# Moving a weight load behind the first z tile, and storing the last zeta in pieces

## The chip, the cores and the metric

The kernel runs on one core of a Trainium2 chip. The metric is device time in microseconds, smaller being better. The engines are named as in the profile: PE (TensorE, matmul), PEld (its weight loads), DVE (VectorE), ACT (ScalarE), POOL (GpSimd) and SP (SyncE, which here only issues DMA transfers).

## The reference

A filter in the frequency domain is followed by a feed-forward layer with squared ReLU:

```
X = rfft(x, axis=1)                     # x: 8 x 3008 x 256
y = irfft(X * (filt_r + 1j*filt_i), n=3008, axis=1)
h = maximum(y.reshape(24064, 256) @ w_in, 0)      # w_in: 256 x 2048
out = (h * h) @ w_out                              # w_out: 2048 x 256
```

## The kernel before

The Fourier transform of length 3008 = 64 x 47 is done as matrix products in stages, in half precision with sums in single precision. For each of the eight batches:

- `unit_a` is the transform over the 47 points (PE, L347), copied out by ACT (L353) and DVE (L359) into tiles `u`, and stored by `write_u` (SP, L330) to the scratch array `dU` in DRAM; `read_u` (SP, L403) reads it back in another layout as `ut`.
- `unit_b` multiplies by the twiddle factors and sums over 32 points (PE, L412, `psB`); DVE multiplies the result by the filter `sF` into `prod` (L420).
- `unit_p` is the first inverse stage (PE, L457, `psP`), copied by ACT into `ze` and stored to the scratch array `dZ`; `read_z` (SP, L475) reads this back as z tiles `zt`, two half tiles for each of four columns c.
- `unit_y` is the last inverse stage (PE, L493, `psY`), copied by ACT (L500) or DVE (L502) into `yt`, the input of the feed-forward layer.

The feed-forward layer works on 47 groups of 512 tokens. `ffn_g1` (PE, L523) multiplies by W_in; ACT applies the ReLU into `h` (L527); DVE squares it (L534). The product with W_out is done for all groups but the last with seven block products (`products`, PE, L638) in place of eight. They need sums of blocks of W_out, made once by `make_t` (DVE, L590), and sums of blocks of `h` for each group (`sums`, DVE, L609 to L618). Both halves of W_out stand in one tile `sWout`, and the first `make_t` reads from both.

In the main loop the steps of one batch's transform lie between the matmuls of the groups before it, in an order that a planner (`fft_plan`) fixes when the kernel is built. Ahead of that loop stands a prologue written out by hand. It has the first batch's transform with nothing to overlap, and then `unit_a` of batch 1. Batch 0 there has a form of its own: `unit_b` writes its twelve products into a ring (`prods`, five slots), and `unit_p0(k)` for k = 0 to 5 takes two of them at a time (PE, L443), which ACT copies (L445) and SP stores (L446). After it follow:

- `read_z(0, 0)` and `read_z(0, 1)`, SP. The first half of a z tile needs the stores of k = 0 to 2, the second half all six.
- a copy of one element of the first z tile on POOL, `tiny` (L790). It does nothing but hold back what stands behind it on POOL until the first half of that tile has landed.
- a load of W_out's second half, `load_wout(1)` (POOL, L321); the first half, `load_wout(0)`, is issued earlier in the prologue, behind the loads of x for batch 1 and ahead of the seven casts of W_in (`cast_win`, L315).
- `unit_a` of batch 1 for c = 0 to 3; its copies stand on ACT and DVE behind the last zeta.
- thirteen matmuls on zeros, the filler (PE, L796), and then `unit_y(0, 0)` to `unit_y(0, 3)`, each with two small matmuls on zeros ahead (L491).

[...] SP's transfers run through one DMA queue (q1 in the profile), POOL's through another (q0), on the same sixteen DMA engines.

Of the kernel before, what the change touches and what calls it, by code (L numbers as in the profile page):

```python
# [110 lines left out]
def kernel(  # L111
# [9 lines left out]
    nc = tc.nc  # L121
    B, S, D = x.shape
# [32 lines left out]
    dZ = [dram.tile([NM * 96, D], F16, name=f"dZ{b}") for b in range(B)]  # L155

    def psF(name):
        return pps.tile([128, 512], F32, tag="psF", name=name, bufs=2)

    def psO(name):  # L160
        return pps.tile([128, 2, 256], F32, tag="psO", name=name, bufs=2)

    def psH(name):
        return pps.tile([128, 2, 512], F32, tag="psH", name=name, bufs=2)
# [21 lines left out]
    def load_x(b, k):  # L186

        c, h = divmod(k, 2)
        if h == 0:
            x16s[(b, c)] = p_x16.tile([112, 8, D], F16, tag="x16", name=f"x16_{b}_{c}")  # L190
        t = x16s[(b, c)]
        n = 48 if b + 1 < B else N2
        v = xrows[b * S:b * S + 64 * n, :].rearrange("(n h m) d -> h n m d", h=2, m=NM)[h]
        for p0, p1 in ((0, n),) if n == 48 else ((0, 32), (32, n)):
            nc.gpsimd.dma_start(out=t[64 * h + p0:64 * h + p1],  # L195
                                in_=v[p0:p1, 8 * c:8 * c + 8, :])
# [24 lines left out]
    def cast(eng, out, in_):  # L221
        (eng.copy if eng is nc.scalar else eng.tensor_copy)(out=out, in_=in_)
# [38 lines left out]
    sF = const.tile([128, 2, NC, D], F16, name="sF")  # L261
    nc.vector.memset(sF[:, 0, 0:2, :], 0.0)
    ps = psO("warm").rearrange("p a d -> p (a d)")
# [49 lines left out]
    def cast_win():  # L313
        for t, k, c in wins:
            nc.gpsimd.tensor_copy(out=sWin[:, k, c], in_=t)  # L315
# [3 lines left out]
    def load_wout(k):  # L319
        c = slice(8 * k, 8 * k + 8)  # L320
        nc.gpsimd.dma_start(out=sWout[:, c, :],  # L321
                            in_=moe_w_out.rearrange("(jt r) c -> r jt c", r=128)[:, c, :])
# [83 lines left out]
    def unit_b(b, p):  # L406
        if b == 0 and p % 4 > 1:
            ps = psO(f"psB_{b}_{p}").rearrange("p a d -> p (a d)")
        else:
            ps = psF(f"psB_{b}_{p}")  # L410
        for i in range(2):
            nc.tensor.matmul(ps[:, i * D:(i + 1) * D], sSB[:, 2 * p + i, :],  # L412
                             uts[b][:, 2 * p + i, :], start=True, stop=True)
        if b == 0:
            if p == 0:
                prods["ring"] = p_y.tile([128, 5, 2, 2, D], F16, tag="yt", name="prods_0")
            prod = prods["ring"][:, p % 5]
        else:
            prod = p_prod.tile([128, 2, 2, D], F16, tag="prod", name=f"prod_{b}_{p}")
        nc.vector.tensor_mul(  # L420
            out=prod,
            in0=ps.rearrange("p (a d) -> p a d", d=D).unsqueeze(1).to_broadcast([128, 2, 2, D]),
            in1=sF[:, :, 2 * p:2 * p + 2, :])
        prods[(b, p)] = prod
        if b > 0:
            for i in range(2):
                nc.gpsimd.dma_start(out=prod[64 * i:64 * i + 64, 0],  # L427
                                    in_=prod[64 - 64 * i:128 - 64 * i, 1],
                                    accum_op=mybir.AluOpType.add)
# [3 lines left out]
    def unit_p0(k):  # L433

        if k == 0:
            zes[0] = p_h2.tile([128, NC, D], F16, tag="h2", name="ze_0")
        ze = zes[0][:, 4 * k:4 * k + 4, :]
        ps = psH(f"psP_0_{k}")
        for i in range(4):
            c2 = 4 * k + i  # L440
            prod = prods[(0, c2 // 2)]
            for v, w in enumerate((sSP[:, c2, :], sSPx[c2 // 12][:, c2 % 12, :])):
                nc.tensor.matmul(ps[:, i // 2, (i % 2) * D:(i % 2) * D + D], w,  # L443
                                 prod[:, v, i % 2, :], start=(v == 0), stop=(v == 1))
        nc.scalar.copy(out=ze, in_=ps.rearrange("p t (a d) -> p (t a) d", d=D))  # L445
        nc.sync.dma_start(  # L446
            out=dZ[0].rearrange("(s p) d -> p s d", p=128)[:, 4 * k:4 * k + 4, :],
            in_=ze)

    def unit_p(b, p):  # L450
        c, i6 = divmod(p, 3)
# [212 lines left out]
    def fft_plan():  # L664

        fixed, units, moves = [], [], []
        for b in range(1, B):
            f = (b * S // TG) * SLOTS - (48 if b > 1 else 40)
            d = 0
            if b == 1:  # L670
                for n in range(4, 16):
                    fixed.append(((n if n < 8 else n + 2 if n < 12 else 2 * n - 7) + n % 2 / 2,
                                  unit_y, 0, n))
                moves.append((7.5, read_z, 0, 3))
                moves.append((0, read_u, b))
                d = 7
            else:
                for a in range(16):
                    if a % 2 == 0 and b > 2:
                        moves.append((f + ((-57 + 2.3 * a) if b == 3 else (-66 + 2.75 * a)),  # L680
                                      load_x, b, a // 2))
                    if a % 4 == 3:
                        units.append((f + ((-13, -9, -5.5, -3)[a // 4], -46 + 2.1 * a, -56 + 2.75 * a)[min(b, 4) - 2],
                                      unit_a, b, a // 4))
                moves.append((f + (2 if b == 2 else -6.5), read_u, b))
            for p in range(12):
                r = 12 + 16.5 * p / 11 if b == 1 else 6 + 28 * p / 11 if b == 2 else -2 + 36 * p / 11
                units.append((f + r, unit_b, b, p))
                if b == 1 and 2 <= p < 10:
                    moves.append((f + r, load_x, 2, p - 2))  # L690
                units.append((f + r + (4.5 if b == 1 else 7 - 2.5 * p / 11), unit_p, b, p))
            for c in range(4):
                moves.append((f + (40 + d / 14, 43, 48, 54)[c] - d, read_z, b, c))
            for n in range(16):
                (fixed if n < 4 else units).append((f + YN[n] - d, unit_y, b, n))
        work, used, done = {}, set(), {}
        for r, *u in fixed:
            h = int(2 * r)
            used.add(h)
            work.setdefault(h, []).append(u)  # L700
        rank = (unit_a, unit_b, unit_p, unit_y)
        for r, *u in sorted(units, key=lambda u: (rank.index(u[1]), u[0])):
            after = done.get((u[0], u[1]), -1)
# [62 lines left out]
    for k in range(6):  # L766
# [5 lines left out]
        if k < 4:  # L772
            load_x(1, 2 * k)
            load_x(1, 2 * k + 1)
    load_wout(0)
    cast_win()
    for k in range(7):
        if k < 6:
            unit_b(0, 2 * k)
            if k < 5:  # L780
                place_f(1, k + 1, nc.scalar)
            unit_b(0, 2 * k + 1)
        if k > 0:
            unit_p0(k - 1)
        if k < 2:
            place_f(0, k + 4, nc.scalar)
# [1 line left out]
    read_z(0, 1)  # L788
    tiny = const.tile([1, 1], F16, name="tiny")
    nc.gpsimd.tensor_copy(out=tiny, in_=ztiles[0][0:1, 0, 0:1])  # L790
    load_wout(1)
    for c in range(4):
        unit_a(1, c)
    ps = psF("fill")
# [11 lines left out]
    for s in range((NG + 1) * SLOTS):  # L806
        g, k = divmod(s, SLOTS)
# [16 lines left out]
        while stores and stores[0][0] <= s:  # L824
            _, i, n, ost = stores.pop(0)
# [31 lines left out]
```

## Time and profile before

| what | value |
|---|---|
| time, median of 4 runs | 760.9 us |
| the four runs | 760.24, 761.57, 761.99, 760.09 us |
| profiled execution | 760.24 us, span 758.4 us |
| granted TensorE clock, mean | 0.995 |
| busy share of the span: PE / DVE / ACT / POOL | 97% / 86% / 74% / 25% |
| chain that ended last, by engine | PE 88%, DVE 5%, DMA 3%, ACT 2% |
| moved by DMA | 106.36 MB, mean 140 GB/s |

The span is the stretch in the trace from the first to the last instruction; the execution's time is 1.84 us longer. All times inside the kernel below are counted from the start of the span. A busy engine need not be the one that decides: what counts in a stretch is which wait ends last there. The shares above are means over the whole kernel, most of which is the main loop, whereas the edits lie in the first 60 us or so, where the stages have other limits.

### The profile page before, as it was taken

Reading aid. Unit: us, or ns where it says so; the run is one execution under the profiler, and the core shown is the slowest. Engines: PE = TensorE matmul, PEld = TensorE weight load, DVE = VectorE, ACT = ScalarE, POOL = GpSimd, SP = SyncE. Lnnn points to the kernel's source line nnn. Section 1 sums busy time; section 2 is a strip of 40 time slices with the busy share of each in tenths; the row PEclk is TensorE's granted clock in tenths of the full one; section 3 lists DMA queues with packets and bytes.
Section 4 is the critical chain, followed back from the end, with each engine's and each line's share of the span. In section 5 each row is a group of like instructions: output and inputs, shape, how many; then the busy total and the mean of one; then the engine's idle time right before and its main releaser. Section 6 shows DMA issues by size and latency. Waiting matters only on the chain.

```text
span 758.4 us, 20196 instructions
## 1 busy us (share of the span) xinstructions
PE 737.9 (97%) x8511; PEld 536.1 (71%) x8511; DVE 655.8 (86%) x729; ACT 564.7 (74%) x807; POOL 190.7 (25%) x265
## 2 busy tenths in 40 slices
PE   7889999999999999999999999999999999999998
PEld 5535666767777777877678776777767777777776
DVE  5859998899899898989979998999988989888783
ACT  5767788777878777787777778777776777777773
POOL 2810750244222321232304224133311222000000
PEclk9899999999999999999999999999999999999999
DMA  9995898666785557746586547754446334321011
GB/s 350 303 203 161 143 182 232 167 115 119 165 221 122 95 129 169 188 103 137 105 208 139 125 99 137 231 127 102 101 119 184 90 71 98 98 84 44 30 57 57
DMA packets 103459, 106.36 MB, mean 140 GB/s; under 512 B 10320, under 2 KB 93520, under 8 KB 102216
## 3 DMA queue, kind: packets, MB, share of 16 engines
q1 hardware_dynamic: 83928, 81.83, 35.9%
q0 software_dynamic: 19296, 23.05, 21.9%
q8 instruction: 67, 1.10, 0.6%
q10 hardware_dynamic: 144, 0.18, 0.1%
q14 instruction: 24, 0.20, 0.1%
HBM read 57.80 MB, written 48.23 MB: 140 GB/s over the span
## 4 chain that ended last, share of the span: by engine, by line
PE 88%; DVE 5%; DMA 3%; ACT 2%; issue 1%; SPq 1%; DVEq 0%; ACTq 0%
PE psH L523 40%; PE psX L638 20%; PE psY L638 16%; PE psB L412 3%; PE psY L493 2%; PE psP L457 2%; PE psA L347 2%; DMA zt<-dZ 2%; DVE prod L420 1%; DMA xw<-in_x_dram 1%; PE psO L543 1%; ACT h L527 1%; DVE h L534 1%; PE psf L286 1%; PE psP L443 1%
## 5 line engine op out<-in xcount | busy, mean ns | idle before, releaser
L527 ACT ACTIVATE h<-psH 128x1024 f16<-128x1024 f32 x376 | 385.0, 1025 | 161.3 <-PE psH L523 160.3
L523 PE MATMUL psH<-yt,sWin 128*128 128x512 f16 (+7 forms) x1728 | 386.8, 351 | 1.2 <-ACT h L527 0.4
L534 DVE TENSOR_TENSOR h<-h 128x2048 f16<-128x2048 f16 (+1 forms) x192 | 229.7, 1197 | 45.5 <-ACT h L527 45.2
L427 POOL DMA_DIRECT2D prod<-prod x168 | 138.7, 968 | 430.6 <-DVE prod L420 428.2
L523 PEld LDWEIGHTS <-sWin 128*128 128x128 f16 x1728 | 149.1, 98 | 90.5 <-issue 3.0
L638 PEld LDWEIGHTS <-sum 128*128 128x128 f16 x2944 | 181.4, 98 | 26.1 <-issue 6.3
L638 PEld LDWEIGHTS <-h 128*128 128x128 f16 x2208 | 135.6, 98 | 24.5 <-issue 5.3
L420 DVE TENSOR_TENSOR prod<-psB,sF 128x1024 f16<-128x1024 f32 x84 | 102.2, 1218 | 11.9 <-PE psB L412 11.8
L638 PE MATMUL psX<-sT,sum 128*128 128x128 f16 x1472 | 104.7, 219 | 0.0
L638 PE MATMUL psY<-sT,sum 128*128 128x128 f16 x736 | 71.2, 219 | 0.0
L638 PE MATMUL psY<-sWout,sum 128*128 128x128 f16 x736 | 56.0, 219 | 1.4 <-DVE bot L653 1.4
L612 DVE TENSOR_TENSOR sum<-sum,h 128x2048 f16<-128x2048 f16 x46 | 56.1, 1220 | 0.8
L638 PE MATMUL psY<-sWout,h 128*128 128x128 f16 x736 | 56.2, 219 | 0.0
L638 PE MATMUL psX<-sT,h 128*128 128x128 f16 x736 | 56.1, 219 | 0.0
L195 POOL DMA_DIRECT2D x<-in_x_dram x64 | 55.8, 1046 | 0.5 <-PE psA L347 0.5
L615 DVE TENSOR_TENSOR sum<-h 128x2048 f16<-128x2048 f16 x46 | 56.0, 1216 | 0.0
L618 DVE TENSOR_TENSOR sum<-h,sum 128x2048 f16<-128x2048 f16 x46 | 55.9, 1216 | 0.0
L609 DVE TENSOR_TENSOR sum<-h 128x2048 f16<-128x2048 f16 x46 | 55.9, 1215 | 0.0
L459 ACT CAST ze<-psP 128x512 f16<-128x512 f32 x84 | 49.2, 586 | 1.2 <-PE psP L457 1.0
L638 PE MATMUL psX<-sWout,h 128*128 128x128 f16 x736 | 48.7, 219 | 0.0
L502 DVE CAST yt<-psY 128x376 f16<-128x376 f32 x62 | 33.6, 542 | 14.8 <-PE psY L493 14.6
L493 PE MATMUL psY<-sC,zt 112*128 112x94 f16 x512 | 42.3, 204 | 3.5 <-DMA zt<-dZ 3.1
(76 smaller groups left out, 545.3 us busy)
## 6 DMA issues: line engine op xcount, KB each, us to landing
zt<-dZ SPq DMA_DIRECT2D x64, 192.0 KB
dU<-u SPq DMA_DIRECT2D x56, 192.0 KB
prod<-prod POOLq DMA_DIRECT2D x168, 64.0 KB, 2.8
dZ<-ze SPq DMA_DIRECT2D x28, 384.0 KB
x<-in_x_dram POOLq DMA_DIRECT2D x48, 192.0 KB, 5.1
ut<-dU SPq DMA_DIRECT2D x7, 1024.0 KB
out_dram<-bot SPq DMA_DIRECT2D x32, 128.0 KB
out_dram<-top SPq DMA_DIRECT2D x16, 256.0 KB
```

The costliest lines, as they stand in the source:

```text
L195: nc.gpsimd.dma_start(out=t[64 * h + p0:64 * h + p1], in_=v[p0:p1, 8 * c:8 * c + 8, :])
L420: nc.vector.tensor_mul(out=prod, in0=ps.rearrange("p (a d) -> p a d", d=D).unsqueeze(1).to_broadcast([128, 2, 2, D]), in1=sF[:, :, 2 * p:2 ...
L427: nc.gpsimd.dma_start(out=prod[64 * i:64 * i + 64, 0], in_=prod[64 - 64 * i:128 - 64 * i, 1], accum_op=mybir.AluOpType.add)
L493: nc.tensor.matmul(ps[:, 94 * jj:94 * jj + 94], zt[:, 4 * (g % 2) + jj, dt * 128:(dt + 1) * 128], sSY, start=True, stop=True)
L523: nc.tensor.matmul(ps[:, i, o:o + n], sWin[:, dt, jt * 128:(jt + 1) * 128], yts[b][:, dt, r:r + n], start=(dt == 0), stop=(dt == 1))
L527: nc.scalar.activation(out=h2[:, 2 * s:2 * s + 2, :], in_=ps, func=AF.Relu)
L534: nc.vector.tensor_mul(out=v, in0=v, in1=v)
L609: nc.vector.tensor_add(out=t, in0=a21, in1=a22)
L612: nc.vector.tensor_sub(out=t, in0=f[5], in1=a11)
L615: nc.vector.tensor_sub(out=t, in0=a11, in1=a21)
L618: nc.vector.tensor_sub(out=t, in0=a12, in1=f[6])
L638: nc.tensor.matmul(o[:, t, :], f[p][:, q, 128 * t:128 * t + 128], sg["w"][p][:, q, :], start=(m == 0 and p in (1, 2)), stop=(q == 7), skip ...
```

## The change

- `load_wout(0)` no longer stands ahead of `cast_win`. Both halves of W_out are issued one after the other behind `tiny`.
- The last product of batch 0 (p = 11) is done by DVE in two instructions of half the width, one for each of its two frequencies' columns, where it was one.
- The last zeta of batch 0 (k = 5) is copied in three pieces: columns 0 and 1 by ACT, column 2 by ACT, column 3 by DVE. Each piece is stored by a transfer of its own. The five zetas before it are copied and stored as they were.

```diff
-        nc.vector.tensor_mul(
-            out=prod,
-            in0=ps.rearrange("p (a d) -> p a d", d=D).unsqueeze(1).to_broadcast([128, 2, 2, D]),
-            in1=sF[:, :, 2 * p:2 * p + 2, :])
+        for a, n in ((0, 1), (1, 1)) if (b, p) == (0, 11) else ((0, 2),):
+            nc.vector.tensor_mul(
+                out=prod[:, :, a:a + n, :],
+                in0=ps.rearrange("p (a d) -> p a d", d=D)[:, a:a + n, :].unsqueeze(1)
+                .to_broadcast([128, 2, n, D]),
+                in1=sF[:, :, 2 * p + a:2 * p + a + n, :])
...
-        nc.scalar.copy(out=ze, in_=ps.rearrange("p t (a d) -> p (t a) d", d=D))
-        nc.sync.dma_start(
-            out=dZ[0].rearrange("(s p) d -> p s d", p=128)[:, 4 * k:4 * k + 4, :],
-            in_=ze)
+        for i, (c0, c1) in enumerate(((0, 4),) if k < 5 else ((0, 2), (2, 3), (3, 4))):
+            cast(nc.vector if i == 2 else nc.scalar, ze[:, c0:c1, :],
+                 ps.rearrange("p t (a d) -> p (t a) d", d=D)[:, c0:c1, :])
+            nc.sync.dma_start(
+                out=dZ[0].rearrange("(s p) d -> p s d", p=128)[:, 4 * k + c0:4 * k + c1, :],
+                in_=ze[:, c0:c1, :])
...
-    load_wout(0)
     cast_win()
...
     nc.gpsimd.tensor_copy(out=tiny, in_=ztiles[0][0:1, 0, 0:1])
-    load_wout(1)
+    for k in range(2):
+        load_wout(k)
```

## The prediction

> **What bounds the kernel now.** I looked first at the clock (0.995 granted), then at the chain of waits, the timeline around the change, the busy time by stage, and the DMA queues by window. The chain of waits from 20 to 90 us (start, duration, what):
>
> ```profile
> 40.88 0.61 PE psP L443 x4
> 41.52 1.02 ACT ze L445
> 42.55 3.57 DMA dZ<-ze
> 46.26 3.09 DMA zt<-dZ
> 50.93 1.18 PE psH L523 x4
> ...
> 59.86 1.08 ACT h L527
> 61.03 1.08 issue
> 62.11 0.69 DVE sT L590
> 62.80 1.14 DVE sum L609
> ```
>
> The last zeta of batch 0 is copied (41.52), stored to `dZ` (landed 46.12) and read back as the first z tile (landed 49.35). Then follow ACT's rectified copies of group 0, and from 62.11 VectorE with `make_t`, which needs all of W_out. The timeline (the bracket is idle time before it and what ended it):
>
> ```profile
> 41.52 1.01 ACT L445 CAST ze<-psP 128x1024 f16<-128x1024 f32 x1 [1.25 <-PE psP L443]
> 42.09 4.62 DVE L359 CAST u<-psA 112x1024 f16<-112x1024 f32 x4 [1.26 <-PE psA L347]
> ...
> 45.08 2.98 PE L796 MATMUL fill<-sSB,zero 128*128 128x512 f16 x13
> 46.83 0.18 POOL L790 COPY tiny<-zt 1x1 f16<-1x1 f16 x1 [7.18 <-DMA zt<-dZ]
> 47.06 0.89 POOL L321 DMA_DIRECT2D sWout<-in_moe_w_out_dram  x1
> ...
> 49.48 0.33 PE L493 MATMUL psY<-sC,zt 112*128 112x94 f16 x4 [1.31 <-DMA zt<-dZ]
> ```
>
> TensorE waits only 1.31 us for the z tile: until 48.17 it runs the 13 filler products and the zeroing ones. Removing DMA time gains no more than that unless the filler moves too. By stage (busy us of PE, PEld, DVE, ACT, POOL; clock; DMA share; GB/s):
>
> ```profile
> 60.00:66.00 6.00, 5.77 (x56) 3.71 (x56) 5.58 (x7) 4.64 (x8) 0.00 (x0) 1.00 0.90 311
> 66.00:72.00 6.00, 5.83 (x70) 4.13 (x68) 6.00 (x8) 3.97 (x6) 0.00 (x0) 1.00 0.13 28
> 72.00:80.00 8.00, 6.21 (x68) 4.50 (x66) 8.00 (x10) 4.22 (x6) 5.60 (x7) 1.00 0.43 76
> 80.00:90.00 10.00, 9.71 (x110) 7.16 (x108) 9.97 (x10) 7.71 (x13) 6.92 (x11) 1.00 0.81 122
> ```
>
> From 66 to 84 VectorE has no gap; after 87 TensorE is 97% busy. A shift of VectorE's start at 62.11 is therefore carried to the end at about 1:1. The DMA queues from 38 to 40 us (packets, MB, share), and W_out's issue to landing:
>
> ```profile
> q0 software_dynamic: 530, 0.27, 112.7%
> q1 hardware_dynamic: 53, 0.03, 5.8%
> ...
> DMA to landing us min/median/max: 8.9/9.0/9.2
> ```
>
> q0 is W_out's first half, q1 the zeta stores: they stand still meanwhile. In the semaphore events of the last zeta store, the eighth of its sixteen engines reports at 44.72 and the last at 46.12; the two stores ahead end at 44.53 and 45.28. The late engines work off a backlog, about 0.8 us a store.
>
> [...] The trace has half clock only from 22.6 to 29.5 us; [...]
>
> **The change, part by part.**
>
> *Product of p = 11 in halves (VectorE).* 1.22 us for 1024 columns and 0.41 for 256 (L653) give some 0.14 fixed and 1.05 ns a column: 0.68 a half, begun 0.62 apart. The pair ends at 40.90, not 40.83. Only the two matmuls of i = 3 then remain (0.27 + 0.11): psP ends near 41.33, not 41.48. Gain 0.15.
>
> *Zeta in three pieces.* In the built program TensorE counts up for this product only at its last matmul. So all three copies wait for the whole of it: halving the product gives nothing more. VectorE's copy also waits for ScalarE's second one. ScalarE: 128x512 takes 0.586 (L459), 128x256 0.37 (L645), begun 0.5 apart: 41.37 to 42.24. VectorE's 256 columns take 0.38 to 0.41: to 42.69. The last store is thus issued at about 42.7, against 42.55: **no gain from the pieces at the issue**. SP has two issues more (0.36 each, the first two beside the copies); `read_z` k = 0 comes at 43.1, where it was 43.84 after a wait for an earlier store. The last piece is 128 packets in place of 512.
>
> *Behind VectorE's piece* stand the four L359 copies of batch 1: first start 42.65, not 42.09, so +0.56. The second of them frees the accumulator of the last `unit_a`, so the filler moves by the same 0.56, to 45.64, and TensorE is free at 48.73 (48.17 before). Bounds: +0.3 to +0.7.
>
> *First W_out load out of 34 to 43 us.* The backlog goes (1.4 us, the span from the eighth engine to the last). The last piece issued at 42.7 lands 1.7 (as the eighth engine did, less 0.6 us of packets) to 2.2 us later: 44.3 to 44.9. The z read then starts near 44.4 where it was 46.26; with its 3.09 it lands at 47.5. Even with the old tail (45.6) it lands at 48.7. TensorE at 48.73 now ends the wait last. **psY starts at 48.75 instead of 49.48: gain 0.73**, bounds 0.4 to 1.0.
>
> *POOL.* The seven W_in casts start 0.95 us earlier (34.3); their user is at 50.9, so this is worth nothing. `tiny` waits for z read k = 0 only, landed near 45.6; W_out's issues stand at 45.7 and 46.6 (0.9 each). Behind them on POOL is nothing until 73.3.
>
> *Both halves landing.* They must be there when VectorE reaches `make_t`: 62.11 - 0.73 = 61.38. First packets come 2.7 us after the issue (as 47.06 to 49.8): 48.4. One half alone costs 3.9 us of the engines (1024 packets at 530 in 2 us), and took 5 to 6 us beside `dU`. Lower bound 48.4 + 7.8 + 0.4 = 56.6; beside `dU` all along 48.4 + 11.3 = 59.7, **which I take**; with nothing overlapped, twice 9.0 from 45.7, 63.7. At 59.7 there are 1.7 us in hand.
>
> *What the second load pushes.* `dU` starts 1.9 us earlier on SP (45.9) and has two or three of its eight stores done before W_out's packets come. I put the end of `dU` (59.9 before) at 59.5 to 61, at worst + 3.9 - 1.4 = 62.4. z tile c = 2 (61.35 before) is then at 61 to 63.8, needed by TensorE at 63.14; a wait of up to 0.7 us there lies beside the stretch in which VectorE is full and TensorE has 1.8 us idle (72 to 80). `ut`'s first piece landed 3.8 us after `dU`, so at worst 66.2, needed at 68.9. Both cost nothing; without that cover, up to 0.7.
>
> *Sum:* -0.73 us. Against the profiled execution: 760.24 (span 758.4 and 1.84 around it) becomes 759.5. It is one of the lower of the four runs; for the median of 760.9, 760.2.
>
> **Rivals.**
>
> (a) *W_out is late* (slower). Both halves share one queue, and the engines are full from 50 to 60 us. It decides from a landing at 61.38 on, and the change loses from 62.11 on. At the upper bound of 63.7 VectorE and the first product of W_out wait: +1.6, 762.5. For it: one half took 9 us; against: most of those are latency and ramp, which two loads in a row pay once.
>
> (b) *More is gained* (faster by over 0.2%). If the copies did start while the second half of the product runs, VectorE's piece would fall into its idle 1.26 us ahead of L359, the filler would start 0.24 earlier than before, and psY at 47.9: -1.55, 759.3. The built waits speak against it. The same happens if the four runs, which lie in two pairs (near 760.2 and near 761.8), meet another mix: 0.8 us from that alone.
>
> (c) *It is eaten.* W_out at 62.1, or z tile c = 2 late by more than TensorE's slack: 0 to +0.4, 761.
>
> **How the numbers follow.** Likeliest: -0.73 with its bounds, 759.8 to 760.7 (0.50); (b) 0.25; (c) 0.10; (a) 0.15. A measurement of this kernel tells about 0.2%, 1.5 us, from no change, and the likeliest case lies inside that. Some of it falls below 759.4 by the spread of runs, so faster is 0.38, same 0.48, slower 0.14. The range takes in (b), (c) and the beginning of (a): 758.6 to 762.2.
>
> **What would show it.** Right: psY near 48.8 with no wait for `zt`; the last zeta store landing by 45; L359 from 42.6 and the filler from 45.6; both W_out landings before 61.4, `make_t` right behind L534. Wrong: VectorE idle before `make_t` with W_out named; TensorE still waiting for `zt` at psY; the filler not later than 45.1; a wait for `zt` or `ut` between 62 and 70 that leaves a gap on VectorE.

## The result, and the profile after

The changed kernel takes 759.29 us (median of 35 runs), the kernel before 760.24 us (median of 56). The ratio is 0.9983, interval 0.9975 to 0.9990: a gain of about 0.2%. The profiled execution took 759.36 us with a span of 757.6, against 760.24 and 758.4.

The chain of waits of the changed kernel around the edits (start, duration, what):

```profile
41.00 0.39 PE psP L445 x2
41.41 0.87 ACT ze L222 x2
42.28 0.02 issue
42.31 0.43 DVE ze L222
42.74 0.04 issue
42.78 0.96 PE psA L347 x8
...
45.46 2.91 PE fill L800 x13
...
50.98 1.03 ACT h L531
52.01 10.37 DMA dU<-u
62.38 0.69 DVE sT L594
```

The store and the read of the last zeta, 3.57 and 3.09 us of the chain before, are gone from it. The filler stands in their place, so psY no longer waits for the z tile. But where the chain before ran over ScalarE's copies of group 0 to `make_t`, there is now one DMA of 10.37 us ahead of it. Its label says `dU`; the timeline tells more:

```profile
43.64 2.42 SPq L479 DMA_DIRECT2D zt<-dZ  x4
...
45.39 2.98 PE L800 MATMUL fill<-sSB,zero 128*128 128x512 f16 x13
...
46.63 0.18 POOL L793 COPY tiny<-zt 1x1 f16<-1x1 f16 x1 [7.75 <-DMA zt<-dZ]
...
46.86 1.83 POOL L321 DMA_DIRECT2D sWout<-in_moe_w_out_dram  x2
...
48.32 0.33 PE L497 MATMUL psY<-sC,zt 112*128 112x94 f16 x4
...
60.96 0.61 PE L642 MATMUL psX<-sWout,h 128*128 128x128 f16 x8
...
62.34 0.61 PE L642 MATMUL psX<-sWout,h 128*128 128x128 f16 x8 [0.78 <-DMA sWout<-in_moe_w_out_dram]
...
62.38 0.69 DVE L594 TENSOR_TENSOR sT<-sWout 128x1024 f16<-128x1024 f16 x1 [1.35 <-DMA dU<-u]
```

psY starts at 48.32 with no bracket, 1.16 us earlier than before. The first product with the first half of W_out starts at 60.96, the next, with the second half, only at 62.34, after a wait that names W_out. VectorE starts `make_t` 0.04 us later. In the semaphore events the second half of W_out lands at 62.30. The `dU` store that lends the second bracket and the chain its name lands only at 62.56, after `make_t` has started, so it is not what `make_t` waited for. All of the lead was lost here, and a little more: `make_t` is at 62.38, where it was 62.11. By stage the hole is plain (columns as in the table by stage before):

```profile
60.00:66.00 6.00, 4.84 (x48) 2.99 (x46) 4.65 (x6) 3.70 (x5) 0.00 (x0) 1.00 0.58 171
66.00:72.00 6.00, 5.87 (x73) 4.37 (x72) 6.00 (x7) 4.08 (x6) 0.00 (x0) 1.00 0.70 255
```

VectorE has 4.65 us in the first stage, and had 5.58.

And yet the span is 0.8 us shorter. How far the kernel is ahead of the kernel before can be followed by the start of the first ReLU copy of each group (ScalarE, `h`), in the two profiled executions:

| at the first ReLU copy of | before | after | difference |
|---|---|---|---|
| group 0 | 52.14 | 50.98 | -1.16 |
| group 1 | 61.50 | 60.29 | -1.21 |
| group 2 | 77.99 | 78.66 | +0.67 |
| group 35 | 578.11 | 578.79 | +0.68 |
| group 36 | 595.05 | 593.80 | -1.25 |
| end of the span | 758.37 | 757.58 | -0.79 |

Three things happen: the lead turns into a lag by group 2; from there to group 35, over 500 us, nothing moves; at group 36 and at the very end the distance changes again, far from the edit. Of the 1.88 us lost between groups 1 and 2, 1.48 are gone at `make_t`. The other 0.40 are not W_out's: before group 2 TensorE waits for a transfer that copies `prod` from one half of its partitions to the other, where the kernel before has no such wait (its line at 76.66 is without a bracket):

```profile
77.33 0.38 PE L461 MATMUL psP<-prod,sSP 128*128 128x256 f16 x2 [0.23 <-DMA prod<-prod]
```

At group 36 it is the kernel before that waits. Its timeline:

```profile
576.82 0.39 PE L638 MATMUL psY<-sWout,sum 128*128 128x128 f16 x4
...
579.90 0.33 PE L493 MATMUL psY<-sC,zt 112*128 112x94 f16 x4 [1.83 <-DMA zt<-dZ]
```

and the same place in the changed kernel, without a bracket:

```profile
577.50 0.39 PE L642 MATMUL psY<-sWout,sum 128*128 128x128 f16 x4
...
578.65 0.33 PE L497 MATMUL psY<-sC,zt 112*128 112x94 f16 x4
```

The tile is z c = 1 of batch 6. Its read is queued on SP behind three stores of `out` and 1.5 MB of `ut`. Whether this wait, and not the prologue, made the measured gain is one of the questions for the experiments.

### The profile page after: what moved, and what is told of

The parts are those of the page before. It is cut to its first block, busy times and chain, and to the rows that moved or that the text cites. A ratio compares the mean times of both kernels' runs of the same rounds, so it can differ in the third digit from the quotient of the medians.

```text
span 757.6 us, 20205 instructions
## 1 busy us (share of the span) xinstructions
PE 738.1 (97%) x8511; PEld 536.0 (71%) x8511; DVE 656.3 (87%) x731; ACT 564.6 (75%) x808; POOL 190.8 (25%) x265
## 4 chain that ended last, share of the span: by engine, by line
PE 90%; DVE 5%; DMA 3%; ACT 1%; issue 1%; SPq 0%; POOL 0%; DVEq 0%; ACTq 0%
PE psH L527 40%; PE psX L642 21%; PE psY L642 16%; PE psB L412 3%; PE psY L497 3%; PE psP L461 2%; PE psA L347 2%; DMA dU<-u 1%; DVE prod L421 1%; DMA xw<-in_x_dram 1%; PE psO L547 1%; PE psf L286 1%; DVE h L538 1%; PE psP L445 1%; DMA prod<-prod 0%
## 5 line engine op out<-in xcount | busy, mean ns | idle before, releaser
L538 DVE TENSOR_TENSOR h<-h 128x2048 f16<-128x2048 f16 (+1 forms) x192 | 229.8, 1197 | 45.6 <-ACT h L531 45.2
```

The source lines that it names most:

```text
L538: nc.vector.tensor_mul(out=v, in0=v, in1=v)
```

## The experiments

Each kernel was timed beside the kernel before on the same chip, and its ratio is to that. There are four sets, each on a chip of its own: the first four experiments, the three with the moved z read, the four on the clock, and the last one. The kernel before took 759.94, 760.15, 760.46 and 761.21 us in them. Times within one set can be compared directly; across sets only roughly.

**The W_out move alone** (`e1_wout_only`).

```
-    load_wout(0)
     cast_win()
...
-    load_wout(1)
+    for k in range(2):
+        load_wout(k)
```

> Only the W_out move; last product and last zeta as before. Theory A (the backlog of the first W_out load was the cost of the zeta store; the pieces add nothing): last zeta store issued near 42.6, landed by 45 (46.12 before), psY at 48.1 to 48.4 (49.48 before, 48.32 with the whole change), L359 from 42.1 and the filler from 45.1. W_out still lands last at 61.5 to 62.8, VectorE waits about 1 us before make_t. Time within 0.1% of the whole change, ratio to before 0.998 to 0.999. Theory B (the pieces bring the gain): psY no earlier than 49.0, and the time at or above before's.

Measured: 757.50 us, ratio 0.9971 (0.9961 to 0.9982), a larger gain than was expected and than the whole change has. The last zeta's store was issued at 43.05 and landed at 45.46, 2.4 us later, where it took 3.57 us with the first W_out load ahead of it. But the profiled execution was one of its slowest (759.89 us) and shows no lead in the prologue: psY is at 49.74, and not at 48.1 to 48.4, as the clock was halved from 44.3 to 47.7 us and the filler took 3.78 us. `make_t` is at 62.38. The wait for W_out that was expected there did not come: it had landed at 60.38.

**The halves and pieces alone** (`e2_pieces_only`): the other two parts of the diff, with `load_wout(0)` in its old place.

> Only the halved product and the three pieces; W_out's halves where they were before. Theory A: the backlog stays, the last piece lands at 45.5 to 46.1, psY at 48.9 to 49.4 (gain 0.1 to 0.6), the second W_out half is in by 57 and nothing waits before make_t; ratio 0.9992 to 1.000. Theory B: psY at 48.3 to 48.5 as with the whole change, and without a late W_out the ratio is 0.998 or lower.

Measured: 760.07 us, ratio 1.0001 (0.9990 to 1.0012). The three pieces land at 45.77 to 46.12, as late as the one store did, and psY is at 49.75, a little later than the 48.9 to 49.4 expected. Alone, they are worth nothing: with the first W_out load in its old place they land no earlier.

**Half of W_out not loaded** (`e3_half_wout`).

```
     cast_win()
+    nc.gpsimd.memset(sWout[:, 8:16, :], 0.01)
...
-    for k in range(2):
-        load_wout(k)
+    load_wout(0)
```

> The whole change with the load of W_out's second half left out (GpSimd fills that half with a constant while it is idle, so half of the product is not the reference's). Theory A (the late second half eats the lead): W_out lands by 58, no wait of VectorE before make_t, which starts at 61.0 (62.38 with the whole change, 62.11 before); group 2 starts 1.0 to 1.2 us ahead of before where the whole change stands 0.67 behind; ratio to before 0.996 to 0.998, below that of the whole change. Rival C (z tile c = 2 or ut, pushed by the loads, would hold VectorE anyway or the main loop gives it back): the wait before make_t goes but the ratio stays at 0.998 to 0.999.

Measured: 760.53 us, ratio 1.0009 (0.9998 to 1.0020). W_out lands at 57.06, `make_t` starts at 60.07 without a wait, and group 2 is 1.95 us ahead of before. About 0.9 of this is clock: this execution had 3.41 us of half clock in place of 6.83, and its last zeta was copied 0.87 us earlier than in the whole change. The rest fits the missing wait: with half of W_out gone, the lead of psY (2.04 us) is still there at `make_t`. So the wait for W_out is what cost the whole change its lead at `make_t`.

But the total isn't lower, against the expectation of 0.996 to 0.998. In its profile the lead goes at 358 us, where TensorE waits for a copy of `prod`,

```profile
358.55 0.38 PE L461 MATMUL psP<-prod,sSP 128*128 128x256 f16 x2 [1.46 <-DMA prod<-prod]
```

and 0.44 more at the end; at 579 us it waits 1.53 us for the z tile, where the kernel before waited 1.83. In this execution the lead was carried 1:1, as the prediction has it, until the next wait for a DMA, and no further. That is one execution; why the median of 14 runs is no better than before is not shown.

**Both W_out loads gated on the first VectorE copy of batch 1** (`e4_gate_on_u`), in place of the z tile.

```
-    nc.gpsimd.tensor_copy(out=tiny, in_=ztiles[0][0:1, 0, 0:1])
-    for k in range(2):
-        load_wout(k)
     for c in range(4):
         unit_a(1, c)
+        if c == 0:
+            nc.gpsimd.tensor_copy(out=tiny, in_=gate[0][0:1, 4, 0:1])
+            for k in range(2):
+                load_wout(k)
```

> The whole change, with the GpSimd copy that holds W_out back waiting for the first VectorE copy of batch 1 (near 43.8) in place of the first z tile (46.6). Theory A: W_out issued near 44.0 and 44.9, landed last at 59 to 60.5, make_t right behind L534 near 61.0 to 61.3; psY at 48.3 to 48.8, since the z read meets W_out's first packets only at its end; ratio to before 0.9965 to 0.998, better than the whole change. Rival D (the gate on the z tile is needed): the z read lands 1 us or more later, psY at 49 or later, ratio 0.999 or more.

Measured: 759.78 us, ratio 0.9994 (0.9979 to 1.0010). W_out is issued at 43.31, has landed by 56.97, and `make_t` doesn't wait; but psY is at 49.16, because the filler ran at half clock here too (44.8 to 48.2, 4.67 us). At 580 us TensorE waits 2.14 us for the z tile, after which the clock halves for another 3.4 us. This execution was the slowest of the 14 (762.72 us). Expected was 0.9965 to 0.998: as in `e3_half_wout`, taking away the wait at `make_t` did not shorten the total, and why is not shown.

**Is the order of the kernels made at 580 us?** In three kernels the read of z tile c = 1 was put directly behind that of c = 0, ahead of the transfers in its way.

```
-                moves.append((f + (40 + d / 14, 43, 48, 54)[c] - d, read_z, b, c))
+                moves.append((f + (40 + d / 14, 43 if b == 1 else 40, 48, 54)[c] - d, read_z, b, c))
```

The kernel before with this move (`f1_before_z`):

> The kernel before, with one move in the main loop: from batch 2 on the read of z tile c = 1 is issued directly behind that of c = 0, ahead of three stores of out and the 1.5 MB ut read of the next batch; the same work is done. In the profiles so far the kernels differ by a constant from group 2 to group 35 and change place at group 36 (580 us), where PE waits for this tile: 1.83 us in the kernel before, 0 in the whole change, 1.0, 0.9, 1.5 and 2.1 in the four experiments. Theory M (the order of the kernels is made by that wait): the wait is gone, and with it 1.5 us: 758.5 (758.0 to 759.0). Theory P (the order is made in the prologue, in runs that the profiles don't show): 759.9 less what all kernels gain equally, at most 0.5: 759.4 to 760.2.

The whole change with it (`f2_after_z`):

> The whole change with the same move of the z read c = 1. Theory M: this kernel had no wait there in its profile, so it gains 0 to 0.4: 759.0 (758.7 to 759.4), and is 0.3 to 0.7 slower than the kernel before with the move, as its prologue was 0.67 behind in the profile. Theory P: it stays 0.9 below the kernel before with the move.

The W_out move alone with it (`f3_wout_z`):

> The W_out move alone (757.5 without this edit) with the same move of the z read c = 1. Theory M: 757.0 to 757.6, within 1 us of the kernel before with the move. Theory P: the distance of 2.4 us to the kernel before stays as it is: 2.0 to 2.8 below the kernel before with the move.

Measured: 758.85 (ratio 0.9985, 0.9976 to 0.9993), 757.82 (0.9964, 0.9952 to 0.9977) and 756.62 (0.9952, 0.9937 to 0.9967). The wait is gone: from group 35 to 36 all three take 14.95 to 14.96 us, where the kernel before took 16.94. And all three gain much the same by it (0.0015 to 0.0019 in the ratio, with intervals of 0.0009 to 0.0015 to each side), so the distances remain: 1.0 and 2.2 us. Theory M has the kernel before right (758.85 lies in its range; theory P allowed it only 0.5 us), but it wants the whole change to be 0.3 to 0.7 slower than it, and that is 1.0 faster: theory M falls as an account of the order. The 1.83 us that the profiled pair differs by at 580 us is chance of one execution; the equal gains say that over many runs every kernel loses time there.

The three profiles also show the prologue a second time. The kernel before has psY at 50.37 and `make_t` at 63.00, 0.9 later than in its first profile. The whole change has psY at 48.29 and `make_t` at 61.96, again after waiting for W_out. The W_out move alone, in an execution without half clock until its last 1.3 us, has psY at 46.64, `make_t` at 59.27, and no wait there.

**Is it the clock?** The three kernels again, with 18 small matmuls on zeros where TensorE waits 1.18 us for the filter, so that the clock might not halve at 22 to 29 us (in the profiles with them it does not: each has at most one piece of half clock, 3.4 us long and after 41 us); and a fourth, with `tiny`'s half tile read earlier.

```
+        for _ in range(fill):
+            nc.tensor.matmul(banks[0][:, 0:128], zero, zero, start=True, stop=True)
...
-    place_f(1, 0, nc.scalar, nc.vector, rotate=True)
+    place_f(1, 0, nc.scalar, nc.vector, rotate=True, fill=18)
```

The kernel before (`g1_before_zc`):

> The kernel before with the moved z read and, in addition, 18 matmuls of 128x128 on zeros ahead of `place_f(1, 0)`, where PE waits 1.18 us for the cast of the filter (21.4 to 22.6 us). In the profiles the clock halves for 3.4 to 6.8 us at 22 to 29 us in eight of nine executions, at a place that differs from one execution to the next; one execution had no half clock and was 2.6 us ahead in group 2. Theory C (the kernels differ in how often the clock halves): without that window this kernel gains 1 to 2 us: 757.3 (756.8 to 758.0). Theory W (they differ in the wait for the z tile and for W_out, whatever the clock): it gains the same 1 to 2 us, as do the others.

The whole change (`g2_after_zc`):

> The whole change with both additions. Theory C: the distance of 1.0 us to the kernel before with the same additions falls to 0.3 or less. Theory W: it stays at 0.7 to 1.3; the profile has make_t 0.9 to 1.4 us behind the first product of W_out's group, waiting for W_out.

The W_out move alone (`g3_wout_zc`):

> The W_out move alone with both additions. Theory C: within 0.5 us of the two others. Theory W: 1.0 to 1.5 below the whole change with the same additions, since W_out lands 0.2 to 2 us ahead of make_t and not 1 us behind it: 755.0 to 755.8.

The whole change with the earlier read (`g4_after_zck`):

```
+        if k == 6:
+            read_z(0, 0, (0,))
         if k > 0:
             unit_p0(k - 1)
...
-    read_z(0, 0)
+    read_z(0, 0, (1,))
```

> The whole change with both additions, and the first half of the first z tile read ahead of the last zeta's stores (it needs those of k = 0 to 2 alone), so that `tiny` and with it both W_out loads come about 2.5 us earlier: issue near 44.2 in place of 46.8, landing near 59.5. Theory W: make_t no longer waits (60.9 in place of 62 on the same clock), and 1.0 to 1.4 us go against the whole change with the same additions; it is then no slower than the W_out move alone. Theory C: no more than 0.3 from the whole change. A third outcome: W_out's first packets reach the last zeta's store or the second half of the z tile, psY is later by 0.5 to 1.5, and the gain is halved.

Measured: 759.96 (ratio 0.9992, 0.9983 to 1.0001), 756.96 (0.9942, 0.9926 to 0.9958), 755.77 (0.9931, 0.9915 to 0.9946) and 757.04 (0.9946, 0.9929 to 0.9963). By the medians, and roughly, as the sets differ, the 18 matmuls are worth 0.9 us to the two kernels with the W_out move (0.0021 to 0.0022 in the ratio) and nothing to the kernel before. The distance from it to the whole change grew from 1.0 to 3.0 us, which neither theory had said: theory C falls, and of theory W only the 1.2 us between the two kernels with the W_out move came as said. The chain of waits of the kernel before with both additions says why:

```profile
38.73 0.61 PE psP L445 x4
39.36 1.02 ACT ze L447
40.40 5.66 DMA dZ<-ze
46.16 0.04 issue
46.20 3.12 DMA zt<-dZ
49.32 0.14 issue
49.45 0.33 PE psY L495 x4
```

The copy of the last zeta starts at 39.36, 2.2 us earlier than in the kernel before. Its store, 3.57 us long there, now takes 5.66, and lands at 46.06, where it landed at 46.12. The 2.2 us that TensorE gains are given to this store, which stands behind the first W_out load on the sixteen engines: the last engine reports that load at 44.29, then three zeta stores follow at 44.55, 45.31 and 46.06. **The kernel before has a floor that DMA sets.** Four profiles have this load in its old place. In them the last zeta is copied at 39.36 to 42.66 and lands at 46.06 to 46.98. With the load moved, one undivided store takes 2.4 to 2.5 us (43.05 to 45.46 in `e1_wout_only`, 40.46 to 42.98 in `f3_wout_z`, 40.65 to 43.15 in `g3_wout_zc`). In this execution TensorE waits 3.43 us for the z tile,

```profile
49.45 0.33 PE L495 MATMUL psY<-sC,zt 112*128 112x94 f16 x4 [3.43 <-DMA zt<-dZ]
```

and half clock follows (the last three columns are TensorE's clock, the DMA share and GB/s):

```profile
44.00:48.00 4.00, 2.02 (x11) 0.88 (x9) 0.55 (x1) 0.28 (x1) 1.07 (x2) 1.00 0.36 118
48.00:50.50 2.50, 1.04 (x22) 1.08 (x23) 0.40 (x1) 0.59 (x2) 0.00 (x0) 1.00 1.03 173
50.50:54.00 3.50, 3.24 (x12) 1.13 (x9) 0.70 (x2) 1.38 (x2) 0.00 (x0) 0.52 1.27 200
```

TensorE does 2.02 of 4.00 and 1.04 of 2.50 us, and in the next 3.4 us runs at half clock, over group 0's first products. The whole change with the same additions has no such place:

```profile
44.00:48.00 4.00, 3.72 (x37) 2.26 (x35) 2.27 (x4) 1.18 (x3) 2.01 (x3) 1.00 1.01 243
48.00:50.50 2.50, 2.25 (x10) 0.87 (x9) 0.14 (x1) 1.46 (x2) 0.00 (x0) 1.00 1.05 155
50.50:54.00 3.50, 3.30 (x19) 1.50 (x18) 2.08 (x2) 3.11 (x4) 0.00 (x0) 1.00 1.32 204
```

In the traces half clock comes in pieces of 3.41 us, one alone or two on end (6.83 us in the kernel before), and where it first begins differs between executions: at 22.6 us in the kernel before, 23.8 in `e1_wout_only`, 24.3 in `e4_gate_on_u`. In `e4_gate_on_u` three pieces begin at 24.31, 44.79 and 580.68: 20.48 and 535.89 us apart, which is 6 and 157 times 3.413. How often a run has next to no half clock (a mean of 0.999 or more) differs between the kernels: none of 161 runs of the kernel before, as it is or with one or both additions; of the W_out move alone 10 of 22, with the moved read 1 of 6, with both additions 5 of 6; of the whole change only 2 of the 36 whose clock is on record, and with the additions 0 of 7 and 4 of 6. Why the whole change as it is has so few is not shown.

Against the W_out move alone, the whole change still waits for W_out. The last column is how far `make_t` starts behind the first product of W_out; the first four rows have the filler at full clock, the last two at half:

| kernel | W_out issued | psY | first product of W_out | W_out landed | `make_t` behind it |
|---|---|---|---|---|---|
| whole change | 46.86 | 48.32 | 60.96 | 62.30 | 1.42 |
| with moved read | 46.78 | 48.29 | 60.93 | 61.88 | 1.03 |
| with both additions | 44.78 | 46.37 | 59.01 | 60.15 | 1.22 |
| W_out alone, moved read | 44.45 | 46.64 | 59.27 | 59.05 | none |
| W_out alone, both additions (filler at half clock) | 44.58 | 47.35 | 59.99 | 59.71 | none |
| whole change, earlier read (filler at half clock) | 42.84 | 47.87 | 60.50 | 56.01 | none |

Both loads need 13.2 to 15.4 us from the first issue. From that issue to the first product the whole change leaves 14.1 to 14.2 us, the W_out move alone 14.8 at full clock and 15.4 at half. That is no wide margin: at full clock W_out came 0.2 us ahead of its use, in one execution. The pieces bring psY 0.3 us forward (46.37 against 46.64 at full clock, where TensorE still waits 0.56 us for the z tile), but not the first half of the z tile, which holds back W_out. The last row shows the wait gone when W_out is issued 1.9 us earlier; but in that execution the clock took it back (filler 4.54 us instead of 2.98, psY 1.5 us later than in the whole change with both additions). The gain of 1.0 to 1.4 us that theory W expected did not come: the median of 757.04 is no better than 756.96. The clock does not explain the median: two of the six runs had no half clock (756.35 and 757.75 us), the other four took 756.59 to 757.18. So none of the three experiments that took the wait for W_out away (`e3_half_wout`, `e4_gate_on_u`, `g4_after_zck`) shortened the total. The wait is seen in the profiles; that it costs the whole change time over many runs is argued, not shown.

**Three copies, one store** (`h1_one_store`): as the whole change with both additions, but the last zeta is stored by one transfer.

```
         for i, (c0, c1) in enumerate(((0, 4),) if k < 5 else ((0, 2), (2, 3), (3, 4))):
             cast(...)
-            nc.sync.dma_start(
-                out=dZ[0].rearrange(...)[:, 4 * k + c0:4 * k + c1, :],
-                in_=ze[:, c0:c1, :])
+        nc.sync.dma_start(
+            out=dZ[0].rearrange(...)[:, 4 * k:4 * k + 4, :],
+            in_=ze)
```

> The whole change with both additions (moved z read, 18 matmuls), but the last zeta, still copied in three pieces, is stored by one transfer as before. It tells why the whole change is 1.2 us slower than the W_out move alone under the same additions (757.0 and 755.8). Theory S (the two extra stores): at the end of the program SP checks eight counters of its transfers in a fixed order; two more transfers move the last store of out from the seventh counter to the first, and all profiles with the pieces have 23.85 us from group 46 to the end in place of 23.38. In addition SP issues the first z read and so W_out 0.4 to 0.6 us later. So this kernel has 23.4 us at the end, and 0.5 to 1.1 less than the whole change with the additions: 755.9 to 756.5. Theory D (the copies: VectorE's piece holds up L359 and the filler): it stays at 756.7 to 757.2 but for the 0.47 at the end, 756.5.

Measured: 756.16 us, beside 761.21 for the kernel before: the ratio is 0.9942 (0.9924 to 0.9960), as for the whole change with both additions. In the total it decides nothing. One part of theory S is seen directly: from group 46 to the end of the span it takes 23.44 us, as in the six other profiles with one store (23.43 to 23.44), whereas the seven with three stores take 23.79 to 24.25. The timelines end like this, before

```profile
755.09 0.37 ACT L554 COPY ost<-psO 128x256 f32<-128x256 f32 x1 [1.33 <-PE psO L543]
```

and after

```profile
753.83 0.37 ACT L558 COPY ost<-psO 128x256 f32<-128x256 f32 x1 [1.33 <-PE psO L547]
```

with the spans ending at 758.37 and 757.58: 3.28 and 3.75 us later. In the built program SP's transfers use eight counters in turn, and its last instructions check them in the order 0 to 7. Before, the last store of `out` is on counter 6, after two transfers more on counter 0, so that six more checks come after it. In the trace they are 0.06 us apart, 0.37 of the 0.47 us. The other part of theory S fell: W_out is issued at 44.59 here and at 44.78 there, 0.2 us and not 0.4 to 0.6, and the last zeta is copied 0.17 us earlier here.

The version with the W_out move alone, the moved z read and the 18 matmuls (755.77 us, ratio 0.9931) is faster than both kernels.

## Why the prediction was right, and where it was wrong

The prediction named the right part of the change: moving the first W_out load gains (0.9971 alone) and the halves and pieces do not (1.0001 alone). The size came out near in part for reasons that it did not give. Step by step:

- **The product in halves** (psP end at 41.33): its last matmul starts at 41.11 and takes 0.27, so 41.38. Right.
- **No gain from the pieces at the issue**: VectorE's piece ends at 42.73 (42.69 was said), L359 follows at 42.65. Right, and the pieces alone measure 1.0001. But the last store was issued at 43.13, not 42.7: SP issued the three at 42.02, 42.62 and 43.13, one behind the other, where the prediction had the first two hidden beside the copies. So the pieces cost 0.6 us at the issue (42.55 before).
- **The W_out backlog goes**: the last piece lands at 44.74 (44.3 to 44.9 was said). Right, and it is what the change is worth. The prediction priced it at 1.4 us of store time in one execution. The runs show it to be more: a floor under the prologue, which in `g1_before_zc` let the last zeta, copied 2.2 us earlier, land only 0.06 us earlier (46.06); and the wait of 3.43 us there was followed by 3.4 us of half clock.
- **The filler's shift** was mis-sized: 0.31 us, the lower bound, where 0.56 was taken. That is 0.25 of the 0.43 us by which psY came earlier than was said (gain 1.16 instead of 0.73).
- **`tiny` and the W_out issue** failed: 46.63 and 46.86, not 45.6 and 45.7. The first z read was put at 43.1 on SP; it stands behind all three stores there and was issued at 43.64. It took 2.94 us to land, as it had before (43.84 to 46.78), where the prediction allowed 2.5.
- **Both halves landing at 59.7, 1.7 us in hand**, is the step that failed: 62.30, inside the bounds but past the need. The issue was 1.2 us later, the loads took 15.4 us where 14.0 were allowed (twice the 9.0 of one load would be 18.0), and the need came at 60.96, 0.4 earlier than was said. From the second half's eighth engine (59.11) to its last (62.30) it took 3.2 us, a tail that this step had not allowed for. `make_t` started at 62.38, 0.08 us behind the last engine; in the kernel before, the z read was issued at 46.26, 0.14 us behind the last engine of the zeta store (46.12). The prediction reckoned with the last engine for that store alone. Rival (a) thus came about in its place, and with its sign at `make_t` only: 0.27 us behind before, not 1.6, since the lead paid for the rest. In size it is nearer to rival (c), W_out at 62.1.
- **`dU` and z tile c = 2**: `dU` ended at 63.13, past its worst case of 62.4, and the tile landed at 64.06, past 63.8. TensorE waited 0.39 us for it at 64.2, while VectorE was full: it cost nothing, as was said.
- **"Carried to the end at about 1:1"** failed in part. From group 2 to group 35 it holds to 0.02 us in this pair. But on the way to group 2 the lag grew from 0.27 to 0.67 at the wait for `prod`, and at 580 us it became a lead of 1.25. Over many runs the wait at 580 us costs all kernels about the same, but the end, with two more transfers, costs 0.47.
- **The sum** of -0.73 was near the measured -0.95 in part for other reasons than given. In the first pair of profiles the lead is eaten by W_out, and the shorter span comes from the wait at 580 us, so the match is partly luck. In the pair with the moved read, where that wait is gone, `make_t` is 1.04 us ahead, and the kernel before has its earliest `make_t` in its first profile: 62.11 there, 63.00 and 63.09 with the additions (psY at 49.48, 50.37 and 49.45). That the change gains in the mean because the kernel before is usually later than in that first profile fits this, but three executions do not show it. How much of the total is the floor, and how much the clock, can be bounded for the W_out move alone: its runs with a mean clock of 0.995, 0.997 and 0.998 took 758.7, 757.8 and 757.8 us (4, 3 and 3 runs), those of the kernel before beside it 759.7, 759.0 and 759.9 (16, 8 and 14). So 1.1 to 2.1 us remain at the same clock.
- **The absolute time**, 759.29, lies below the likeliest 759.8 to 760.7, since the median of the kernel before turned out at 760.24 and not 760.9. Two sums of the prediction are off by a little: 760.9 less 0.4 to 1.0 is 759.9 to 760.5, and 2.17 less 0.6 is 1.6, not 1.7 (the 0.6 is an estimate: 24 packets fewer on each engine, at 27 ns for one of q1's in the trace of the kernel before). Neither matters here.

Three things stay open: what makes the last engines of W_out's load 0.7 to 3.2 us later than the eighth; why the copy of `prod` was late at 358 us in `e3_half_wout`, which no other profile has; and why taking away the wait for W_out never shortened the total.

## What to carry to other kernels

A bulk load that runs beside small stores on a critical path can set a floor under them, as the first W_out load did here: the last zeta, copied at 39.36 to 42.66, landed at 46.06 to 46.98 in the four profiles with it, and at 42.98 to 45.46 without it as one store. Move it behind them first, and ask then when it has to land, counted from the issue to the last engine (15.4 us here), not to the eighth (12.2). Splitting the store helped nothing while that load was there (ratio 1.0001), and the two parts more cost 0.6 us at the issue and 0.47 us at the end. One profiled execution of a kernel with half clock and DMA waits is a sample (`make_t` at 62.11, 63.00 and 63.09 in the kernel before, as it is and with the additions): take two or three before a difference of a microsecond is explained by it.

## What was not expected of the hardware

- A wait for a transfer was paid twice where TensorE's clock halved afterwards: 2.14 us at 580 us in `e4_gate_on_u`, then 3.41 us at half clock, and group 35 to 36 took 18.90 us, where 14.96 is the time without a wait. It did not always halve: after the 1.83 us at the same place in the kernel before it did not, and 16.94 was the time.
- Thirteen filler matmuls that took 2.98 us at full clock took 3.77 to 4.67 where the clock halved under them. They didn't prevent it. In the five executions where this was seen, TensorE was busy for 2.2 to 2.4 of the 3.41 us just ahead.
- The same two transfers of W_out, 0.5 MB each as written, took 8.6 to 10.6 us (first) and 12.2 to 14.5 us (second) from their issues, in the nine profiles that have the two in a row.
